# Products with w1 read the first norm's transposed tile, with the second norm's factor per token applied behind them

## The chip, the cores and the metric

The kernel runs on one core of a Trainium2 chip. Its time is the device time of one execution in microseconds (us). Five engines work side by side, each in the order of its own queue: TensorE (PE, matrix products, with the weight loads listed as PEld), VectorE (DVE), ScalarE (ACT), GpSimd (POOL) and SyncE (SP, which here issues most DMA transfers). They wait for one another by semaphores.

## What is computed

x holds 2,048 tokens of 512 values. It is normalised once (xn), and xn goes two ways: through an attention with 32 heads of 16 in four segments of 512 tokens, and through an MLP of width 1,792 that normalises xn a second time.

```
def _A_ref(x, wq, wk, wv, wo, beta):
    ...
    for s in range(N):
        qs, ks, vs = q[:, :, s], k[:, :, s], v[:, :, s]
        logits = jnp.einsum("bhqd,bhkd->bhqk", qs, ks) * scale + mask
        p = _softmax(logits, axis=-1)
        a_dot = jnp.einsum("bhqk,bhkd->bhqd", p, vs)
        pq = phi(qs)
        num = jnp.einsum("bhld,bhde->bhle", pq, M)
        den = jnp.einsum("bhld,bhd->bhl", pq, z)[..., None] + 1e-6
        o = g * (num / den) + (1.0 - g) * a_dot
        ...
    return o @ wo

def _B_ref(x, w1, b1, w2, b2):
    y = _layernorm(x, axis=-1)
    h = _gelu(jnp.einsum("bsd,df->bsf", y, w1) + b1)
    return jnp.einsum("bsf,fd->bsd", h, w2) + b2

xn = _layernorm(x, axis=-1)
return x + _A_ref(xn, ...) + _B_ref(xn, ...)
```

A row of xn already has mean zero. Its second norm is therefore xn times one number per token, which depends on the variance of the row of x alone.

## The kernel before

Precision: every float32 operand of the large products is split into two float16 parts, high and low, and a product is the sum of three (high-high, high-low, low-high), so `split3` (L499) issues 12 products for a contraction over 512.

Work is cut into segments of 512 tokens (s, 0 to 3), groups of 8 heads (g, 0 to 3; i = 4s + g counts 16 of them), halves of 256 tokens (hf, 0 to 7) and halves of the hidden width (fh; j = 2 hf + fh counts 16 MLP stages of 7 blocks of 128 columns).

The jobs that the prediction speaks of:

- `ln` (L462) and `ln_out` (L477). For kind "X" they load two token tiles of x, compute the statistics on DVE (`norm_stats`), apply them on POOL or ACT (`norm_apply`), transpose them on PE (four transposes for each tile, L490) and split them into `xnT[s]`, one buffer for 512 tokens. For kind "Y" they load the same tiles of x again, compute the statistics again, apply both norms at once (the second pair in `stats`), and transpose into `yT`, a tile for 256 tokens.
- `qk_proj` (L517): projection of a group's queries or keys, 12 products of 512 columns, read out by ACT and by DVE (`qk_low`), stored to memory, and reloaded by `qk_rows` in another layout (`qst`, `kst`).
- `m_job` (L637): score products whose row maxima DVE takes (L653); `m_row` (L657) transposes the maxima, stores them (`md`) and `max_rows` adds them to `qst`. `s_job` (L677): the scores again, with the maximum subtracted, and their exponentials on ACT (L695, `pt`). `s_mask` masks on POOL, `pv` (L716) multiplies with the values, `o_norm` divides.
- `d_jobs` (L773): a block of 128 hidden columns for 256 tokens, 12 products of 256 columns with `yT`; the result is scaled and b1 added while it is read from PSUM, on ACT for even blocks and on DVE for odd ones (`Z_ON`), into `hT`. `gelu` (L790): one ACT instruction over the seven blocks, 1,792 columns. `h_split` (L795) splits the result, and `e_jobs` (L815) multiply with w2.
- `out_jobs` (L840): the products with wo. `v_nat` (L606): the values.

PSUM has eight banks of 512 float32 columns. Which bank a job takes is written out in `BANKS`, and the order in which all jobs are issued in `ORDER`: one character for each job, which names the stream (`streams`, L58) whose next job follows. Each engine gets its instructions in that order. ACT needs one table set for exponentials and another for the gelu; `plan` (L167) places the reloads, one before and one after each of the 16 gelu stages.

Of the kernel before, what the change touches and what calls it, by code (L numbers as in the profile page):

```python
# [19 lines left out]
P = 128  # L20
# [30 lines left out]
Z_ON = "AVAVAVA"  # L51
# [6 lines left out]
def streams():  # L58
# [76 lines left out]
    "egaeaaeRgeaRTTaTTeaaRTebeebScbbTcfXXTUecSUhVdeegXdijUUZWZZe3lZm001y0YY0k21k23l0ImI1I30IVeoY0o21IIeY44e52IJ4Ao6"  # L135
    "o54hKNcWo4Le6Oo75ioA4AoMkKooL764P75PMUjVKkLAP7o6Mz7#nPKLUyPM8PP89!Po8ppP9WII8!8NqppoIeqPopoqX#O#I8rr9rreop!oPP"
    "89Ip!opIpqo#IoopPccqz#rrqrJrod$$%$KdP$shInp&%Ni&pIjLaMlmt$aqkpp$kuqplvI%IqIyIwo(eoxor$rrrpPmPKLIppoaM&KzqPoL%p"
    "OohMqoopPPiaK(qP&koLJMoKrr(LrMrPPsPKojtbkbIPLnIP(PMKPIupopLIDvI)wPpqoMapNIopoPPxqaqyKPIrrLOrarppoPPzoaMo*oJPKP"
    "bPbPL)qPcP+MP)copohipjpPoPcd*dqlnCqyrKm)rrrLpppsq+MhkIItuIkpoKpvwIELqPiFqDooMKrrrxrGLPIjPPoppHlpoMpPPPIpokoICq"
    "qPIPmJoookqrrrKrPAPLPsootnooAuPopvMpwxPqAppqpAEoorrqrrKpopBpooBpQLMqpKcNqcoBoPnBLqrrrrpcpzsytquhvjPMpOKipFpPGq"  # L140
    "IHlQzmIDwqIxrrCNrLrppOpMkkPPPIIpoqoPIdydpooEqahoiQooJqkrrrrsPPIKLMIPotKuovoPPLPFIPIPjowMGKLxHMKlILNPnmkIPMpppa"
    "PIPqPOzPPoJaopaPPPbKqICPLMpooPbPqrQKLrrMroDopIIopoIKLPNPMaIpppaqIqKLEIqooararrrPPJosbybtMPPPOunhvPpppjccFiPGcw"
    "HPPqpKqpqPLPlxkmdMzdrrrCKrppPyhpLkppDjqIiEIqIoqorMrrroosoKAAtooIAuvowoFoGHIxLkloBICMInKPpmpQkApppPPqqPzPLcJqoo"
    "oDrrrrBpMpoPPKLyoopBppohooqMqorqrrriBPPoIsntjEPPQPuPvppFGpHkwcKILlzmPqMPPNpkpCKqxILQINIyrrqrrMoopPDIIKpoPdcOLo"
    "ppMPqOPPqpooPPqdPoJKaorrLrroosMhIEiKLtMQuNIPPvojFKIGLkHPPPnMlPPmwKIppIPLqxPppMpPCazIPykIoqaJooqPPrKDrrrooLMoPN"
    "KPIbILpapoPPPbPppaoMPPoqpoOOqPaIrKrqrrosaEaLMKIIInPtbbIcuLpppvPhpFcipcDGqHqldCMmPdPPwPPqJrrxrKkrcpppPkPhPEiqIo"
    "ppLzIqooqorrrMKrsPAooLMKotuvIAocwooFLPIGMHlIICIoKPnxBAAmpppLkBPkooqphPopMoQPJqPiPPrqKrrroooPPBppLMKoPNIOpoqPPQ"
    "oDLpNpBoIIMqqrKrrLrnppsqpMtcIKIIIEupvpFPwLOPqGHqlmPdCdxPJPkrrMrrppPkPPPKPPopLoqMPPIpKpqoIqPorrrLMDrsoooKEtuhIP"
    "PQiIvPoLMoFoKQLwGPkHlmIMoIIJPPDKPLMPPInCkIpKpqoxPPpoPPppoqILooqrrrropPpMoNKqIppoqLIooMNpKILOIorrqrrsMJnPKPtOPE"
    "upppPPppPPvwqLPqqPrFxrrrpMKpGPPPLqPMKpppPHLqPPPqMrrrKLrsMPPtPPPPuPvPwPxPPBBBBQQQQ"  # L150
# [4 lines left out]
    "01234567012345601274350617243150627341502734015273401576340123470162347062134076213407612340761243607124731602"  # L155
    "47316524763015247630524763052467310246170234610724671204671254361725431672453016742350617452061207465120746352"
    "40673540267315420731654273164527136527136075123062531064251032641703264170326417304173265041732650417326045173"
    "20645173245061725407612407561240561724056172406517243605127403612740326740326710452610452610453610543617043561"
    "72043175620147356214735162473516243750243175043217043521670432156701432657014321657043216570432167543210754321"
    "07542310754231072534610374256104237610423760452376045236145723614527345612735461352476015324701532470152470315"  # L160
    "67031564703154672031546723154673215421673052310673521067235016723501672530167524316752430617542310675423106542"
    "35106423510645210643521064352130564103564720356472037526403527106435271063452671043526710325674103264710326043"
    "721560403721506472150647150632715207631205726031572601357426013754021637524106375410637542106754210367154"
# [17 lines left out]
def infini_mixer_kernel(ctx: ExitStack, tc: tile.TileContext, x, wq, wk, wv, wo, beta, w1, b1, w2, b2, out):  # L181
# [240 lines left out]
    stats = cst.tile([P, S // P, 2, 2], F32, name="stats")  # L422

    def norm_stats(tok, tiles):


        n = len(tiles)
        ag = sm.tile([P, 4, 2], F32, name="ag", bufs=1)[:, :n]
        for j, t in enumerate(tiles):
            st = sm.tile([P, 6], F32, name="st")  # L430
            V.bn_stats(st, t)
            V.bn_aggr(ag[:, j, :], st)
        w = sm.tile([P, 3, 4, 2], F32, name="nw", bufs=1)[:, :, :n]
        a, y, b = w[:, 0], w[:, 1], w[:, 2]
        r = stats[:, tok:tok + n]
        V.tensor_scalar(a[:, :, 0], ag[:, :, 1], EPS, None, op0=OP.add)
# [5 lines left out]
        q = r[:, :, :, 0]  # L442
# [6 lines left out]
        for j in range(2):  # L449
            V.scalar_tensor_tensor(r[:, :, j, 1], ag[:, :, 0], -1.0, r[:, :, j, 0], op0=OP.mult, op1=OP.mult)  # L450

    def norm_apply(tok, tiles, twice, act, j):
        for t in tiles[j:j + 1]:
            a, b = stats[:, tok + j, twice, 0:1], stats[:, tok + j, twice, 1:2]
# [7 lines left out]
    def ln(kind, n, b, part):  # L462

        tok = 4 * n + 2 * b if kind == "X" else 2 * n
        if part == 0:
            lt[kind, n, b] = ts = []
            for j in range(2):
                name = ("nN", "nD")[j] if (kind, n, b) == ("X", 0, 1) else "xt"
# [3 lines left out]
        elif part == 1:  # L472
            norm_stats(tok, lt[kind, n, b] + (lt[kind, 0, 1] if n == 0 else []))
        else:
            norm_apply(tok, lt[kind, n, b], kind == "Y", (kind, n, b) == ("X", 0, 1), part - 2)

    def ln_out(kind, n, b, k):  # L477
        if kind == "X":
            if n not in xnT:
                xnT[n] = sb.tile([P, KT, 2, SEG], F16, name="xnT")  # L480
            ln_tr(lt["X", n, b][k], xnT[n], 256 * b + P * k)
        else:
            if n not in yT:
                yT[n] = sb.tile([P, KT, 2, 256], F16, name="yT")
            ln_tr(lt["Y", n, b][k], yT[n], P * k)

    def ln_tr(t, dst, c0):
# [8 lines left out]
    xnT = {}  # L496
    yT = {}

    def split3(p, parts, n, s0, s1):  # L499

        (ws, wsl), (xs, xsl) = parts
        i = 0
        for k in range(n):
            for a, b in ((0, 0), (0, 1), (1, 0)):
                T.matmul(p, wsl(ws, k, a), xsl(xs, k, b), start=s0 and i == 0, stop=s1 and i == 3 * n - 1)  # L505
# [11 lines left out]
    def qk_proj(i, which):  # L517
# [3 lines left out]
        split3(p, ((w, lambda w, k, a: w[:, g, a, P * k:P * k + P]),  # L521
                   (xnT[s], lambda t, k, a: t[:, k, a, :])), KT, True, True)
# [83 lines left out]
    def v_nat(s, b):  # L606
        p = dense()
        split3(p, ((xnT[s], lambda t, k, a: t[:, k, a, P * b:P * b + P]),
                   (wvs, lambda w, k, a: w[:, k, a, :])), KT, True, True)
# [163 lines left out]
    def d_jobs(j):  # L773
        hf, fh = divmod(j, 2)
        hz = hzs[fh]

        def f(fi):
            def go():
                fo = FH * fh + fi
                p = dense()  # L780
                split3(p[:, :256], ((WT["1"], lambda w, k, a: w[:, fo, a, P * k:P * k + P]),
                                    (yT[hf], lambda t, k, a: t[:, k, a, :])), KT, True, True)
                if Z_ON[fi] == "A":
                    A.activation(hz[:, fi, :], p[:, :256], AF.Identity, bias=b1t[:, fo:fo + 1], scale=col(CG + fh))  # L784
                else:
                    V.tensor_scalar(hz[:, fi, :], p[:, :256], col(CG + fh), b1t[:, fo:fo + 1], op0=OP.mult, op1=OP.add)  # L786
            return go
        return [f(fi) for fi in range(FH)]

    def gelu(j):  # L790
        A.activation(hzs[j % 2], hzs[j % 2], AF.Gelu_apprx_tanh)  # L791
# [100 lines left out]
    def e_of(j, a, f):  # L892
# [8 lines left out]
        "X": lambda *k: ln("X", *k), "Xt": lambda *k: ln_out("X", *k),  # L901
        "Y": lambda *k: ln("Y", *k), "Yt": lambda *k: ln_out("Y", *k), "gate": gates,
        "D": lambda j, f: once("D", j, lambda: d_jobs(j))[f](),
# [38 lines left out]
```

## Time and profile before

| | us |
|---|---|
| median of three runs | 722.24 |
| the three runs | 720.87, 722.24, 722.72 |
| the profiled execution | 720.38 |
| its span, first to last instruction | 718.7 |

The profile is one execution. In its lists, a line gives the place in the kernel (L505 is line 505, often that of a helper), the engine, the operation, the tiles out<-in, the size, and the count; then the busy time in us and the mean of one in ns; then the idle time of the engine just before such instructions and what ended most of it. A list of waits gives the engine and line that waited, for whom, the us in total, how often, and the longest. A timeline gives start, duration, engine, line and tiles, with the idle time in brackets. The duration of a product includes its way through the array, which overlaps the next one; the pace is read from the starts.

### The profile page before, as it was taken

What the parts mean: (1) busy time and instruction counts of PE and PEld (TensorE: products, weight loads), DVE (VectorE), ACT (ScalarE), POOL (GpSimd) and SP (SyncE); (2) the same over time, 40 slices, a digit from 0 to 9 for tenths busy, and PEclk for the clock granted to TensorE, in tenths of its full rate; (3) what the DMA queues carried; (4) which work ended last, traced back from release to release, by engine and by line L of the source; (5) the groups of instructions that cost most, each with busy time, mean ns of one, the idle gap of its engine ahead of it and who ended that gap; (6) DMA issues with size and microseconds to landing.
All of it is one profiled execution on the core that took longest, in us unless ns stands there. A gap on an engine that the chain in (4) does not pass through costs nothing.

```text
span 718.7 us, 14578 instructions
## 1 busy us (share of the span) xinstructions
PE 689.8 (96%) x5189; PEld 379.0 (53%) x5189; DVE 524.3 (73%) x1677; ACT 519.7 (72%) x908; POOL 352.9 (49%) x544
## 2 busy tenths in 40 slices
PE   2799999999999999999999999999999999999997
PEld 2365655564554465665555456556556455455543
DVE  5799877988786659897485866888658484696642
ACT  5989998889767577578936757676864567748980
POOL 3568746655514462654533336445634245334572
PEclk9999999999999999999999999999999999999999
DMA  9886124503220163322313024322240321322101
GB/s 266 242 255 157 53 79 108 127 16 92 52 68 3 61 148 89 82 53 55 96 31 90 16 66 113 92 60 60 68 104 2 97 67 17 82 68 68 32 1 59
DMA packets 54084, 59.16 MB, mean 82 GB/s; under 512 B 5038, under 2 KB 40892, under 8 KB 54012
## 3 DMA queue, kind: packets, MB, share of 16 engines
q1 hardware_dynamic: 51708, 54.04, 27.0%
q0 software_dynamic: 2304, 4.20, 3.6%
q8 instruction: 41, 0.67, 0.4%
q14 instruction: 31, 0.25, 0.1%
HBM read 41.18 MB, written 17.04 MB: 81 GB/s over the span
## 4 chain that ended last, share of the span: by engine, by line
PE 84%; DMA 5%; ACT 5%; DVE 2%; issue 2%; SPq 1%; POOL 0%; POOLq 0%; DVEq 0%; ACTq 0%
PE dense L505 33%; PE dense L831 19%; PE dense L722 9%; PE dense L646 6%; PE dense L688 5%; PE dense L849 5%; DMA qst<-qd 2%; DMA qd<-hl 2%; PE dense L601 2%; PE dense L589 1%; PE dense L621 1%; PE dense L490 1%; ACT pt L695 1%; DMA pt<-in_A_wq_dram 1%; PE dense L562 1%
## 5 line engine op out<-in xcount | busy, mean ns | idle before, releaser
L653 DVE CUSTOM_DVE_ANT_0 dense<-dense,mask 128x384 f32<-128x384 f32 (+3 forms) x512 | 234.0, 524 | 37.9 <-PE dense L646 35.8
L695 ACT ACTIVATE pt<-dense,qkcs 128x512 f32<-128x512 f32 (+1 forms) x384 | 204.4, 628 | 28.0 <-PE dense L688 27.9
L831 PE MATMUL dense<-w2s,hT 128*128 128x512 f16 x672 | 165.3, 380 | 0.0
L505 PE MATMUL dense<-yT,w1s 128*128 128x256 f16 x1344 | 160.5, 273 | 1.8 <-POOL w1s L413 1.4
L709 POOL TENSOR_SCALAR_AFFINE_SELECT pt<-pt 128x256 f32<-128x256 f32 x256 | 102.7, 443 | 104.5 <-ACT pt L695 104.0
L505 PEld LDWEIGHTS <-w1s 128*128 128x128 f16 x1344 | 129.5, 98 | 34.7 <-issue 9.9
L805 POOL TENSOR_TENSOR hT<-hh,hT 128x512 f16<-128x512 f32 x64 | 69.5, 1086 | 64.6 <-ACT hT L803 61.9
L831 PEld LDWEIGHTS <-hT 128*128 128x128 f16 x672 | 60.9, 98 | 71.3 <-issue 16.7
L722 PE MATMUL dense<-pt,vt 128*32 128x512 f32 (+3 forms) x1024 | 76.3, 436 | 0.0
L653 DVE DVE_READ_ACCUMULATOR2_ANT mc<- 128x1 f32 x512 | 71.9, 140 | 0.0
L801 POOL TENSOR_SCALAR hh<-hT,sc 128x512 f32<-128x512 f32 x64 | 43.4, 679 | 46.7 <-ACT hT L791 43.6
L784 ACT ACTIVATE hT<-dense,b1t,sc 128x256 f32<-128x256 f32 x64 | 36.7, 573 | 37.8 <-PE dense L505 37.3
L753 POOL TENSOR_TENSOR nN<-nN,oT 128x512 f32<-128x512 f32 x16 | 20.5, 1280 | 73.8 <-DVE oT L574 73.8
L646 PE MATMUL dense<-kst,qst 48*128 48x384 f16 (+3 forms) x512 | 52.7, 298 | 3.8 <-DMA qst<-qd 3.8
L722 PEld LDWEIGHTS dense<-pt,vt 128*32 128x32 f32 x1024 | 30.9, 109 | 45.2 <-issue 33.4
L688 PE MATMUL dense<-qst,kst 50*128 50x384 f16 (+3 forms) x512 | 52.1, 298 | 2.1 <-DMA qst<-md 1.7
L505 PE MATMUL dense<-xnT,wks 128*128 128x512 f16 x192 | 45.6, 388 | 0.0
L505 PE MATMUL dense<-xnT,wqs 128*128 128x512 f16 x192 | 44.1, 379 | 0.0
L849 PE MATMUL dense<-wos,oT 128*128 128x512 f16 x192 | 43.8, 379 | 0.1
L505 PE MATMUL dense<-wvs,xnT 128*128 128x512 f16 x192 | 43.6, 379 | 0.0
L803 ACT ACTIVATE hT<-hh 128x512 f16<-128x512 f32 x64 | 37.4, 584 | 7.4 <-POOL hh L801 7.4
L786 DVE TENSOR_SCALAR hT<-dense,sc,b1t 128x256 f32<-128x256 f32 x48 | 25.9, 539 | 23.0 <-PE dense L505 22.8
(223 smaller groups left out, 931.5 us busy)
## 6 DMA issues: line engine op xcount, KB each, us to landing
xt<-in_A_x_dram SPq DMA_DIRECT2D x30, 256.0 KB
kd<-hl SPq DMA_DIRECT2D x48, 128.0 KB
qd<-hl SPq DMA_DIRECT2D x48, 128.0 KB
kst<-kd SPq DMA_DIRECT2D x32, 192.0 KB
qst<-qd SPq DMA_DIRECT2D x32, 192.0 KB
acc<-in_A_x_dram SPq DMA_DIRECT2D x16, 256.0 KB
acc<-in_B_b_dram POOLq DMA_DIRECT2D x16, 256.0 KB, 4.1
out_dram<-acc SPq DMA_DIRECT2D x16, 256.0 KB
```

The costliest lines, as they stand in the source:

```text
L505: T.matmul(p, wsl(ws, k, a), xsl(xs, k, b), start=s0 and i == 0, stop=s1 and i == 3 * n - 1)
L646: T.matmul(p[:, o:o + n], stk[i, 0][r, t, P * qb:P * qb + P], stk[i, 1][r, t, :n], start=True, stop=True)
L653: V.tensor_tensor_reduce(p[:, o:o + n], p[:, o:o + n], mask[:, 512 - n:], 1.0, -3e38, OP.add, OP.max, mc[i][:, 4 * b + t, qb:qb + 1])
L688: T.matmul(p[:, o:o + n], stk[i, 1][r, t, P * kb:P * kb + P], stk[i, 0][r, t, P * kb:], start=True, stop=True)
L695: A.activation(pt[i, 4 * b + t][:, OFF[kb]:OFF[kb] + n], p[:, c:c + n], AF.Exp, scale=qkcs[:, 1, i % NG:i % NG + 1])
L709: G.affine_select(v, v, pattern=[[0, 2], [1, P]], compare_op=OP.is_ge, fill=0.0, base=0, channel_multiplier=-1)
L722: T.matmul(p[32 * c:32 * c + 32, P * kb:], vt[s, kb][:, 4 * g + c, 16 * odd:16 * odd + 32], pt[i, 2 * c + odd][:, OFF[kb]:OFF[kb] + LEN[kb ...
L801: G.tensor_scalar(hht[j, c], hz[:, z, :], col(SHH + j % 2), 0.0, op0=OP.mult, op1=OP.add)
L803: A.activation(hT[:, z, 0, :], hht[j, c], AF.Copy)
L805: G.tensor_tensor(hT[:, z, 1, :], hht[j, c], hT[:, z, 0, :], op=OP.subtract)
L831: T.matmul(p, t[:, u, P * a:P * a + P], w2s[:, fo, v, :], start=fi == 0 and n == 0, stop=fi == FH - 1 and n == 2)
L849: T.matmul(p, o[:, u, P * b:P * b + P], wos[:, g, v, :], start=i == 0, stop=i == 3 * NG - 1)
```

## The change

The second transposed tile is gone. The products with w1 read the first norm's tile, and what the second norm would have multiplied each token's row with, one factor per token, is applied when the products are read from PSUM.

- The streams "again" and "againt" (second load, statistics, norm and transposes) become "ratio" and "ratio2". `ratio` works out the factor for the 256 tokens of a half from what `norm_stats` left (two small DVE products) and stores it to memory; `ratio_rows` loads it back as a row of 256 that stands in all 128 partitions (`cb`, one buffer).
- `xnT` becomes a ring of three halves of 256 tokens. A segment's two halves are neighbours in it for segments 0, 2 and 3, not for segment 1, whose query and key projections are issued as two times 12 products of 256 columns (`x_seg`).
- Two blocks of w1 products share one PSUM bank, and one DVE instruction multiplies both with the scale and with the factors. The last of the seven blocks stands alone.
- b1 is added inside the gelu, as its bias column, which takes one ACT instruction for each block, seven in place of one.
- The first loads change place (x first), and `ORDER` and `BANKS` are written anew.

```diff
-Z_ON = "AVAVAVA"
...
-    for n in range(2 * NSEG):
-        put("again", *[("Y", n, 0, k) for k in (0, 2, 3)])
-        put("againt", *[("Yt", n, 0, k) for k in range(2)])
+    for h in range(2 * NSEG):
+        put("ratio", ("C", h))
+        put("ratio2", ("Cb", h))
...
-    stats = cst.tile([P, S // P, 2, 2], F32, name="stats")
+    stats = cst.tile([P, S // P, 2], F32, name="stats")
+    nws = {}
...
+    def ratio(h):
+
+        w, o = nws[2 * h]
+        a, q = w[:, 0, o:o + 2], w[:, 3, o:o + 2]
+        t = sm.tile([P, 2], F32, name="cr", bufs=1)
+        V.tensor_tensor(t, a[:, :, 0], q[:, :, 0], op=OP.mult)
+        V.tensor_tensor(t, t, q[:, :, 1], op=OP.mult)
+        Q.dma_start(cd[h].rearrange("t p -> p t"), t)
+
+    def ratio_rows(h):
+        cbt[h] = sb.tile([P, 256], F32, name="cb")
+        Q.dma_start(cbt[h], bass.AP(tensor=cd[h].tensor, offset=cd[h].offset, ap=[[0, P], [1, 256]]))
...
+    xnT = cst.tile([P, 3, KT, 2, 256], F16, name="xnT")
+
+    def ln_out(n, b, j):
+        t, dst, c0 = lt[n, b][j], xnT[:, (2 * n + b) % 3], P * j
...
+    def x_seg(s):
+
+        a, b = 2 * s % 3, (2 * s + 1) % 3
+        if b == a + 1:
+            return [(slice(0, 512), lambda k, u: xnT[:, a:a + 2, k, u, :])]
+        return [(slice(256 * j, 256 * j + 256), lambda k, u, h=h: xnT[:, h, k, u, :]) for j, h in enumerate((a, b))]
...
-    def d_jobs(j):
+    dp = {}
+
+    def d_job(j, f):
         hf, fh = divmod(j, 2)
...
+        fo = FH * fh + f
+        if f % 2 == 0:
+            dp[0] = dense()
+        p = dp[0]
+        split3(p[:, 256 * (f % 2):256 * (f % 2) + 256], lambda k, a: WT["1"][:, fo, a, P * k:P * k + P],
+               lambda k, a: xnT[:, hf % 3, k, a, :])
+        if f % 2 or f == FH - 1:
+            f0, n = f - f % 2, 1 + f % 2
+            V.scalar_tensor_tensor(hzs[fh][:, f0:f + 1, :], p[:, :256 * n].rearrange("p (f c) -> p f c", f=n), col(CG + fh),
+                                   cbt[hf].unsqueeze(1).to_broadcast([P, n, 256]), op0=OP.mult, op1=OP.mult)
 
     def gelu(j):
-        A.activation(hzs[j % 2], hzs[j % 2], AF.Gelu_apprx_tanh)
+        for f in range(FH):
+            fo = FH * (j % 2) + f
+            A.activation(hzs[j % 2][:, f, :], hzs[j % 2][:, f, :], AF.Gelu_apprx_tanh, bias=b1t[:, fo:fo + 1])
```

More of the change, by code (lines that the diff above doesn't have):

```diff
@@ L472, in ln @@
         elif part == 1:
-            norm_stats(tok, lt[kind, n, b] + (lt[kind, 0, 1] if n == 0 else []))
+            norm_stats(tok, lt[n, b] + (lt[0, 1] if n == 0 else []))
         else:
[L475 to L487, printed above, removed]
+            norm_apply(tok, lt[n, b], (n, b) == (0, 1), part - 2)
+    xnT = cst.tile([P, 3, KT, 2, 256], F16, name="xnT")
+    def ln_out(n, b, j):
+        t, dst, c0 = lt[n, b][j], xnT[:, (2 * n + b) % 3], P * j
         p = dense()
@@ L494, in ln_tr, with x_cols, split3 @@
         V.scalar_tensor_tensor(dst[:, :, 1, c0:c0 + P], p3, 1024.0, h, op0=OP.mult, op1=OP.subtract)
[L496 to L501, printed above, removed]
+    def x_seg(s):
[3 more added lines that the diff above has]
+        return [(slice(256 * j, 256 * j + 256), lambda k, u, h=h: xnT[:, h, k, u, :]) for j, h in enumerate((a, b))]
+    def x_cols(s, b, k, u):
+        return xnT[:, (2 * s + b // 2) % 3, k, u, P * (b % 2):P * (b % 2) + P]
+    def split3(p, ws, xs):
         i = 0
-        for k in range(n):
+        for k in range(KT):
             for a, b in ((0, 0), (0, 1), (1, 0)):
-                T.matmul(p, wsl(ws, k, a), xsl(xs, k, b), start=s0 and i == 0, stop=s1 and i == 3 * n - 1)
+                T.matmul(p, ws(k, a), xs(k, b), start=i == 0, stop=i == 3 * KT - 1)
                 i += 1
@@ L607, in v_nat @@
         p = dense()
[L608 to L609 removed]
+        split3(p, lambda k, a: x_cols(s, b, k, a), lambda k, a: wvs[:, k, a, :])
         t = vts[b]
```

98 lines of the change are left out of this document (44 added, 54 removed).

## The prediction

> **What bounds the kernel now.** I read the page's busy times first, then the table by stage, then what TensorE (PE) waits for, then the timeline of a quiet stretch.
>
> ```profile
> PE 689.8 (96%) x5189; PEld 379.0 (53%) x5189; DVE 524.3 (73%) x1677; ACT 519.7 (72%) x908; POOL 352.9 (49%) x544
> ...
> PEclk9999999999999999999999999999999999999999
> ```
>
> PE is busy for 689.8 of 718.7 us at a full granted clock. A busy PE need not be a PE at its peak, so the next rows matter more. The columns of the table by stage are the stage, then busy time and count for PE, weight loads, DVE, ACT and POOL, then clock, DMA share and GB/s.
>
> ```profile
> 0.00:20.00 20.00, 6.01 (x24) 4.77 (x25) 11.23 (x47) 12.31 (x27) 7.69 (x21) 1.00 0.91 267
> 20.00:40.00 20.00, 15.36 (x94) 9.38 (x93) 15.83 (x50) 18.53 (x32) 12.13 (x13) 1.00 0.75 224
> ...
> 300.00:320.00 20.00, 20.00 (x171) 11.99 (x170) 17.00 (x66) 16.69 (x27) 10.32 (x17) 1.00 0.38 92
> ...
> 600.00:620.00 20.00, 18.89 (x132) 9.70 (x129) 10.14 (x12) 18.29 (x30) 11.75 (x18) 1.00 0.36 78
> ```
>
> In the first 20 us DMA is the full resource (0.91), in the next 20 ACT (18.53). Later PE fills the stage, with a small hole at 600. What the holes are:
>
> ```profile
> PE dense L490 <- POOL xt L458: 7.4, 1, 7.4
> PE dense L359 <- ACT wqs L343: 6.4, 2, 5.6
> PE dense L646 <- DMA qst<-qd: 3.8, 5, 1.1
> PE dense L376 <- ACT w1s L343: 3.1, 1, 3.1
> PE dense L688 <- DMA qst<-md: 1.7, 1, 1.7
> PE dense L505 <- POOL w1s L413: 1.4, 1, 1.4
> ```
>
> The 7.4, 6.4, 3.1 and 1.4 are the start. After it, PE waits 5.5 us (3.8 + 1.7) for two DMA chains. Whether it is at its peak between them shows in the starts of neighbouring jobs:
>
> ```profile
> 300.62 1.47 PE L505 MATMUL dense<-yT,w1s 128*128 128x256 f16 x12
> 301.93 1.46 PE L831 MATMUL dense<-w2s,hT 128*128 128x512 f16 x6
> ...
> 306.26 2.12 PE L831 MATMUL dense<-w2s,hT 128*128 128x512 f16 x9
> 308.22 0.60 PE L490 MATMUL dense<-ident,xt 128*128 128x128 f32 x4
> 308.65 1.47 PE L505 MATMUL dense<-yT,w1s 128*128 128x256 f16 x12
> ```
>
> Twelve products of 256 columns take 301.93 - 300.62 = 1.31 us (109 ns each), nine of 512 take 308.22 - 306.26 = 1.96 us (218 ns each): the pace follows the columns and no weight load shows. Four transposes take 308.65 - 308.22 = 0.43 us. So from about 36 us on, time is PE's own work, and only an edit to that work, or to the 5.5 us of waits, is on the path.
>
> **PE's work, part by part.** The second norm's tile is gone: 8 halves of two 128-token tiles, so 16 groups of four transposes, 16 x 0.43 = **-6.9 us**. The products with w1 keep count and shape (1,344 of 256 columns): 0. In the ring, segment s lies in slots 2s and 2s+1 modulo 3; only segment 1 lies in slots 2 and 0. There the 8 query and key projections split from 12 products of 512 columns into 24 of 256. A 512-column projection takes 2.59 us (606.48 to 609.07, quoted below), the split one 2 x 1.31 = 2.62: 8 x 0.03 = **+0.2 us**. The other segments, and the value products, which read 128 columns at a time, keep their shapes.
>
> **What lies beside PE.** The rows that price it:
>
> ```profile
> L784 ACT ACTIVATE hT<-dense,b1t,sc 128x256 f32<-128x256 f32 x64 | 36.7, 573 | 37.8 <-PE dense L505 37.3
> ...
> L791 ACT ACTIVATE hT<-hT 128x1792 f32<-128x1792 f32 x16 | 27.2, 1698 | 0.2
> ...
> L786 DVE TENSOR_SCALAR hT<-dense,sc,b1t 128x256 f32<-128x256 f32 x48 | 25.9, 539 | 23.0 <-PE dense L505 22.8
> ...
> L458 POOL TENSOR_SCALAR xt<-xt,stats 128x512 f32<-128x512 f32 x30 | 24.0, 802 | 18.0 <-DVE stats L450 6.3 <-PE dense L505 4.5 <-DVE wks L407 3.7
> L835 DVE SCALAR_TENSOR_TENSOR acc<-dense,sc,acc 128x512 f32<-128x512 f32 x32 | 23.9, 746 | 18.8 <-PE dense L831 18.5 <-DMA qd<-hl 0.2
> ...
> L791 ACT ACT_TABLE_LOAD x16 | 20.5, 1283 | 0.3
> ...
> L494 DVE SCALAR_TENSOR_TENSOR yT<-dense,yT 128x512 f16<-128x512 f32 x16 | 10.8, 682 | 3.9 <-ACT yT L493 3.9
> L431 DVE BATCH_NORM_STATS2 st<-xt 128x6 f32<-128x512 f32 x14 | 9.4, 674 | 5.8 <-DMA xt<-in_A_x_dram 5.8
> L493 ACT ACTIVATE yT<-dense 128x512 f16<-128x512 f32 x16 | 9.1, 601 | 0.7 <-PE dense L490 0.7
> ...
> L803 ACT ACTIVATE hT<-hh 128x256 f16<-128x256 f32 x16 | 6.8, 423 | 2.5 <-POOL hh L801 2.5
> ```
>
> ```profile
> 300.86 0.17 DVE L436 TENSOR_SCALAR nw<-ag 128x2 f32<-128x2 f32 x1
> ...
> 303.37 0.23 DVE L450 SCALAR_TENSOR_TENSOR stats<-ag,stats 128x2 f32<-128x2 f32 x2
> ```
>
> DVE loses the 48 reads of L786 (25.9), the 16 of L494 (10.8), and eight repeats of the statistics: two reads of 0.67 and a chain of 303.60 - 300.86 = 2.7, about 4.1 each, 33. It gains 64 products with the factor per token: 48 of 512 columns at L835's 0.746 and 16 of 256 at L786's 0.54, 44.4, and 16 small ones at 0.17 for the factor: 2.7. Net 47.1 - 69.7 = -23 us. The new form (PSUM times a row repeated over two blocks) is not in the trace; below, 0.539 for a plain 512-column read would be kind, above, a quarter over 0.746 costs 9 us more and still leaves DVE under its present load. I take 0.746, the same operation.
>
> ACT loses L784 (36.7), L493 (9.1) and 16 wide gelus (27.2), and gains 112 gelus of 256 columns with a bias column. Their price lies between L803's 0.423 (same size, SBUF, no column) and L784's 0.573 (PSUM, two columns): 47 to 64 us; I take 0.45, nearer the SBUF row, 50, net -23. POOL loses 16 x 0.80 = 12.8. The cover is that PE reads none of these directly. If it is gone, each gelu stage is 7 x 0.423 - 1.70 = 1.3 to 7 x 0.573 - 1.70 = 2.3 us longer with ACT closed to everything else. Against that, the wide gelu starts only when all seven products are read; a slice starts when its own two are, so behind the last product remain a DVE read, one slice and the table reload, 0.54 + 0.45 + 1.28 = 2.3, where there were 0.57 + 1.28 + 1.70 + 1.28 = 4.8. In the order string the gelu now mostly stands 0 to 5 us behind its last product, formerly up to 17. I take 0.
>
> The Trainium skill speaks against the slices: "ScalarE: Activation LUTs", section "What ACT_TABLE_LOAD costs", gives an activation with a bias column a fixed 280 ns and 0.833 ns per column, and 186 ns fixed without it. By it the wide gelu is an estimated 1.68 us, with which the row (1.698) agrees, and seven slices 3.45 us; that is inside the bounds above, leaves the sum, and would make the slower rival below 16 x 1.8 = 28 us instead of its 21.
>
> **Queues and added waits.** SP issues 16 second reads of x less and 16 small transfers more: the factors of a half are stored to memory and come back repeated over all partitions. The load back waits on SP for its store, and for the last DVE product of the half before, as it has one buffer; behind it wait the projection stores and reloads that feed the maximum products. The nearest row for such a pair is the maxima's round trip:
>
> ```profile
> SPq L669 <- DMA md<-mhl: 18.5, 15, 2.2
> ```
>
> That is 18.5 / 15 = 1.2 us mean. In the new order most factors are stored some 30 us of PE work or more ahead of the load, so I take 0; eight full waits would be 10 us of SP, not of PE. Of the ring: the tile of half h+3 overwrites that of half h, so its copies on ACT and DVE now wait for the w1 jobs of half h too. In the new string these stand 55 us of PE work ahead at the least, so 0; out of order they would hold the next segment's projections. Two w1 jobs share a PSUM bank, so their read starts up to 1.31 us later; the bank's next use stands no nearer behind it than before (0.65 us at the least in both strings): 0.
>
> **The new order.** I laid both strings out with PE prices from the rows. Two places where PE waited:
>
> ```profile
> 589.74 0.27 PE L659 MATMUL dense<-ident,mc 128*32 128x128 f32 x1
> ...
> 596.65 0.98 PE L688 MATMUL dense<-qst,kst 50*128 50x512 f16 x8 [1.73 <-DMA qst<-md]
> ...
> 606.48 2.75 PE L505 MATMUL dense<-xnT,wqs 128*128 128x512 f16 x12
> 609.07 0.81 PE L831 MATMUL dense<-w2s,hT 128*128 128x512 f16 x3
> ...
> 611.98 2.36 PE L722 MATMUL dense<-pt,vt 128*32 128x512 f32 x32
> 614.27 0.61 PE L688 MATMUL dense<-qst,kst 50*128 50x512 f16 x6
> 614.81 4.06 PE L831 MATMUL dense<-w2s,hT 128*128 128x512 f16 x18
> ...
> 620.89 0.39 PE L646 MATMUL dense<-kst,qst 48*128 48x512 f16 x1 [0.53 <-DMA qst<-qd]
> ```
>
> From the end of a query projection (609.07) to its maximum products (620.89) the chain needs 11.8 us. The old string put 9.5 us of PE work between them; the new one puts three w1 jobs, nine of w2, one value group and two score jobs there: 3.93 + 5.85 + 2.29 + 0.54 = 12.6. The shortest such distance over the 16 groups is 8.7 in the old, 10.9 in the new. From the maxima's transpose (589.74) to the scores (596.65) the chain needs 6.9; the old string had 4.9 there, the new one 6.8, least 5.6 against 4.1. So of the 5.5 us of waits I take **-4**, with bounds of -5.5 and 0. A new order can also place new waits that I don't see: **+2**, from 0 to 8.
>
> **The start.** x is now read ahead of the first weights, and the second read is gone:
>
> ```profile
> 14.72 1.16 SPq L470 DMA_DIRECT2D xt<-in_A_x_dram  x2
> ...
> 18.95 4.19 PE L505 MATMUL dense<-xnT,wks 128*128 128x512 f16 x12
> ```
>
> The row at 14.72 stood ahead of w1: 0.5 MB at 267 GB/s is 1.9 us. The first weights come 1 MB, 3.9 us, later, the norms 1.9 earlier. The first projection (18.95) needs both. I take **-1**, from -3 (norms and w1 both earlier, within the 4.5 us of L376's and L413's waits) to +4 (all of the weights' delay).
>
> **Sum.** 718.7 - 6.9 + 0.2 - 4 + 2 - 1 = 709.0 us of span; with the 1.7 us around it (720.38 - 718.7) 710.7. The profiled execution lies 1.9 under the median of the runs, so 712.6 against 722.24. The likeliest case's own range is 707 to 717.
>
> **Rivals.** (1) More: waits wholly gone, no new ones, start -3: 722.24 - 6.9 + 0.2 - 5.5 - 3 = 707. For it, the wider distances; against it, the old string had such waits at distances that looked long enough.
> (2) Given back: the new order's waits come to 8 and the old ones change places (0 gained): 722.24 - 6.7 + 8 - 1 = 722.5. For it, DVE alone now reads the w1 products, and it is near full at places (17.00 of 20 at 300); against it, it carries 23 us less.
> (3) Slower: the slices hold ACT, the scores' exponentials queue behind them, their PSUM banks stay taken and PE stops at the next score job. With 1.3 us exposed in all 16 stages, 712.6 + 20.8 = 733. It decides from 12 us on, that is from nine stages. For it, the score jobs that in the new string follow three gelus within 3 us; against it, the earlier start of the slices.
> (4) That the transposes stood in time that PE would have waited anyway is excluded by the rows at 306 to 308, which touch.
>
> **Chances.** Forecast 0.60, (1) 0.12, (2) 0.12, (3) 0.16. Differences within 0.3% (2.2 us) can hardly be told from no change here. (2) is half of that kind and splits the rest: faster 0.75, same 0.06, slower 0.19. The range, 705 to 723, leaves out (3) and the ends of the others.
>
> **What would show it.** No transposes of xt beyond the first norm's 64 and PE's work about 6.7 us less; waits for qst under 2 us; ACT's gelu rows near 0.45 us and no PE wait on L695; DVE's busy time near 500. PE waits for ACT's or DVE's readers of PSUM adding to over 10 us would prove the forecast wrong, as would a first projection later than 22 us.

## The result and the profile after

The changed kernel takes 742.28 us (median of 4 runs, 741.61 to 746.31) against 721.56 us (4 runs, 719.76 to 722.72) of the kernel before in the same session: 1.0301 times, 95% interval 1.0258 to 1.0345. The forecast was 712.6, so the sign was wrong. The profiled execution spans 739.9 us where before it was 718.7.

The page of the changed kernel, busy times, granted clock (tenths of full speed in 40 slices) and packets:

```profile
PE 700.2 (95%) x5221; PEld 383.9 (52%) x5221; DVE 528.8 (71%) x1693; ACT 501.1 (68%) x924; POOL 338.9 (46%) x528
...
PEclk9989999999999999999999899999899999999999
...
DMA packets 55110, 56.04 MB, mean 76 GB/s; under 512 B 7086, under 2 KB 43964, under 8 KB 55036
```

PE is busy 10.4 us longer than before (689.8), though 64 transposes are gone, and three slices of the clock show an 8 where there was none. Outside its busy time PE idles 739.9 - 700.2 = 39.7 us, before 718.7 - 689.8 = 28.9. The table by stage says where (stage, then busy time and count of PE, weight loads, DVE, ACT, POOL, then clock, DMA share, GB/s):

```profile
20.00:40.00 20.00, 13.44 (x47) 5.39 (x47) 11.16 (x44) 12.73 (x22) 5.71 (x6) 0.85 0.77 162
100.00:120.00 20.00, 17.61 (x127) 10.24 (x126) 12.90 (x37) 15.31 (x28) 9.48 (x14) 0.91 0.26 73
280.00:300.00 20.00, 18.35 (x141) 10.73 (x140) 17.27 (x49) 11.30 (x21) 5.30 (x12) 0.91 0.27 63
300.00:320.00 20.00, 20.00 (x152) 14.21 (x151) 14.91 (x45) 10.92 (x21) 10.16 (x11) 1.00 0.48 135
400.00:420.00 20.00, 16.78 (x117) 7.50 (x115) 8.85 (x29) 8.39 (x16) 3.11 (x8) 0.83 0.17 47
520.00:540.00 20.00, 16.17 (x93) 8.32 (x86) 10.05 (x18) 12.63 (x24) 5.75 (x7) 0.83 0.11 29
```

The stage at 300 is as full as before. The loss lies in a few places, the start among them (13.44 us of PE work at 20 to 40, 15.36 before). At 400 and 520 the other engines do less as well and DMA moves little (47 and 29 GB/s): what is waited for is neither large nor starved, but late. (The stage at 280 has another cause, which the last experiment takes up.) The waits of PE and of SP's queue in the changed kernel (engine, line, for whom, us in total, times, longest):

```profile
PE dense L704 <- DMA qst<-md: 7.3, 3, 3.7
...
SPq L685 <- DMA md<-mhl: 27.2, 13, 6.8
...
SPq L468 <- DMA cd<-cr: 16.2, 2, 8.8
```

Before, SP's longest wait for the maxima's store was 2.2 us; now it is 6.8. SP waits up to 8.8 us for the new store of the factors (`cd`). The timeline of the changed kernel shows what the two have in common:

```profile
27.39 0.42 SPq L464 DMA_DIRECT2D cd<-cr  x1
27.86 0.45 SPq L311 DMA_DIRECT2D w2s<-in_B_w_dram  x1
37.17 0.34 SPq L468 DMA_DIRECT2D cb<-cd  x1
...
98.60 0.38 SPq L464 DMA_DIRECT2D cd<-cr  x1
106.47 0.33 SPq L468 DMA_DIRECT2D cb<-cd  x1
...
521.47 0.38 SPq L464 DMA_DIRECT2D cd<-cr  x1
...
523.37 0.33 SPq L680 DMA_DIRECT2D md<-mhl  x1
...
530.57 0.56 SPq L685 DMA_DIRECT2D qst<-md  x2
...
532.26 1.99 PE L704 MATMUL dense<-qst,kst 50*128 50x512 f16 x8 [3.69 <-DMA qst<-md]
```

At 98.60 the factors are stored and come back at 106.47, 7.9 us later. At 521.47 they are stored again, and 1.9 us behind them the maxima; now the maxima need 7.2 us (523.37 to 530.57), though the load of the factors only stands behind them. So the store is late itself and what is issued behind it is late too. At the start the store at 27.39 comes back 9.8 us later (37.17), and a load of weights goes out right behind it. The stage of 30 to 32 us, in the changed kernel and in the version with rows below (t_rows), which has the same load at 27.61:

```profile
30.00:32.00 2.00, 2.00 (x9) 0.83 (x9) 1.56 (x12) 1.37 (x2) 0.00 (x0) 0.69 1.34 32
```

```profile
30.00:32.00 2.00, 2.00 (x7) 0.72 (x6) 1.70 (x12) 1.09 (x4) 0.86 (x2) 0.52 0.96 363
```

The DMA share is high in both (1.34 and 0.96), but what moves is 32 GB/s behind the scattered store and 363 without it: data are held up, and not only the news that they have landed. The first products with w1 start at 38.30 there, at 33.22 in t_rows.

At 530 PE pays twice. Stages of the changed kernel around that place, same columns:

```profile
524.50:529.50 5.00, 4.07 (x20) 1.67 (x18) 3.09 (x7) 2.83 (x5) 2.48 (x3) 1.00 0.03 3
529.50:532.50 3.00, 0.24 (x1) 0.09 (x1) 0.43 (x1) 0.00 (x0) 1.37 (x2) 1.00 0.04 7
532.50:539.40 6.90, 6.76 (x22) 3.23 (x22) 1.69 (x3) 5.32 (x9) 0.00 (x0) 0.51 0.25 77
```

PE stands still for most of 3 us, and then works 6.9 us at a granted clock of 0.51: another 3.4 us lost without any wait in a list (after 539.4 the clock is full again). Over the span, the clock's mean of 0.979 makes 0.021 x 739.9 = 15 us of it.

### The profile page after: what moved, and what is told of

It is laid out like the page before. It is cut to its first block, busy times and chain, and to the rows that moved or that the text cites. A ratio compares the mean times of both kernels' runs of the same rounds, so it can differ in the third digit from the quotient of the medians.

```text
span 739.9 us, 14673 instructions
## 1 busy us (share of the span) xinstructions
PE 700.2 (95%) x5221; PEld 383.9 (52%) x5221; DVE 528.8 (71%) x1693; ACT 501.1 (68%) x924; POOL 338.9 (46%) x528
## 4 chain that ended last, share of the span: by engine, by line
PE 71%; DMA 8%; ACT 6%; issue 5%; DVE 5%; POOL 4%; SPq 1%; POOLq 0%; ACTq 0%; DVEq 0%
PE dense L522 29%; PE dense L847 14%; PE dense L738 8%; PE dense L865 5%; PE dense L662 5%; PE dense L704 5%; DMA md<-mhl 2%; DMA kd<-hl 2%; DMA qst<-qd 1%; ACT pt L711 1%; PE dense L618 1%; PE dense L606 1%; PE dense L637 1%; DMA wqs<-in_A_wq_dram 1%; PE dense L579 1%
## 5 line engine op out<-in xcount | busy, mean ns | idle before, releaser
L522 PE MATMUL dense<-xnT,w1s 128*128 128x256 f16 x1344 | 166.4, 276 | 5.6 <-ACT w1s L410 3.9
L847 PE MATMUL dense<-w2s,hT 128*128 128x512 f16 x672 | 169.1, 384 | 0.3 <-ACT pt L711 0.2
L801 DVE SCALAR_TENSOR_TENSOR hT<-dense,sc,cb 128x512 f32<-128x512 f32 x64 | 43.4, 680 | 37.6 <-PE dense L522 33.1
L704 PE MATMUL dense<-qst,kst 50*128 50x384 f16 (+3 forms) x512 | 54.4, 301 | 7.8 <-DMA qst<-md 7.3
L662 PE MATMUL dense<-kst,qst 48*128 48x384 f16 (+3 forms) x512 | 54.4, 302 | 4.6 <-DMA qst<-qd 1.8
L542 ACT ACTIVATE hl<-dense 128x512 f16<-128x512 f32 x32 | 19.1, 598 | 46.0 <-PE dense L522 32.5
L807 ACT ACTIVATE hT<-hT,b1t 128x256 f32<-128x256 f32 x112 | 47.2, 496 | 4.3 <-DVE hT L801 3.8
L522 PE MATMUL dense<-xnT,wqs 128*128 128x512 f16 (+1 forms) x240 | 47.3, 352 | 0.0
L522 PE MATMUL dense<-xnT,wks 128*128 128x512 f16 (+1 forms) x240 | 46.2, 347 | 1.0 <-ACT wks L405 1.0
```

The lines of the kernel that those rows point to most:

```text
L522: T.matmul(p, ws(k, a), xs(k, b), start=i == 0, stop=i == 3 * KT - 1)
L662: T.matmul(p[:, o:o + n], stk[i, 0][r, t, P * qb:P * qb + P], stk[i, 1][r, t, :n], start=True, stop=True)
L704: T.matmul(p[:, o:o + n], stk[i, 1][r, t, P * kb:P * kb + P], stk[i, 0][r, t, P * kb:], start=True, stop=True)
L801: V.scalar_tensor_tensor(hzs[fh][:, f0:f + 1, :], p[:, :256 * n].rearrange("p (f c) -> p f c", f=n), col(CG + fh), cbt[hf].unsqueeze(1).to ...
L807: A.activation(hzs[j % 2][:, f, :], hzs[j % 2][:, f, :], AF.Gelu_apprx_tanh, bias=b1t[:, fo:fo + 1])
L847: T.matmul(p, t[:, u, P * a:P * a + P], w2s[:, fo, v, :], start=fi == 0 and n == 0, stop=fi == FH - 1 and n == 2)
```

## The experiments

My theory: the store of the factors, 256 pieces of 4 B in the order "t p -> p t", is late, and holds what is issued behind it. Rivals: the new order, and the gelu slices. The first four runs tell them apart. Two of them leave the second norm's factor out, as their expectations say.

**The factors as rows (t_rows).** DVE transposes the factors in blocks of 32, so that a store has pieces of 128 B. Everything else, order, slices and ring, is that of the changed kernel.

```diff
-        t = sm.tile([P, 2], F32, name="cr", bufs=1)
+        w = mst[:, 3] if h < 2 else ones
+        t, r = w[:, 0:2], w[:, 32:64]
...
-        Q.dma_start(cd[h].rearrange("t p -> p t"), t)
+        V.transpose(r, w[:, 0:32])
+        for c in range(2):
+            Q.dma_start(cd[h][c].rearrange("(b k) -> b k", k=32), r[c:P:32, :])
```

> The changed kernel, but the factors of a half are transposed on DVE in blocks of 32 and stored as eight pieces of 128 bytes in place of 256 pieces of 4 bytes. In the profile of the changed kernel the scattered store at 98.60 us let its reload go only at 106.47, and the maxima stored at 523.37, right behind another such store, could be read back only at 530.57, 7 us instead of the usual 1.5. Theory A (the scattered store completes some 7 us late and holds what is behind it): the waits of PE for the maxima fall from 7.3 us to under 2, the drops of the granted clock behind them go, time 719 to 729. Rival B (the new order is short of distance whatever the store is): 739 to 745, the same waits. Rival C (the gelu slices hold ACT): also 739 to 745.

Measured: 713.1 us (4 runs, 711.87 to 714.83), 0.9913 of the kernel before (0.9881 to 0.9944), 6 us under the expected range. Page and timeline of this kernel:

```profile
PE 689.4 (97%) x5221; PEld 380.3 (53%) x5221; DVE 530.6 (74%) x1701; ACT 501.0 (70%) x924; POOL 338.9 (48%) x529
```

```profile
90.71 1.09 SPq L467 DMA_DIRECT2D cd<-mst  x2
93.56 0.33 SPq L471 DMA_DIRECT2D cb<-cd  x1
```

Store to reload takes 2.9 us instead of 7.9, and PE waits for no `qst` at all. PE's busy time falls by 10.8 us (the clock) and its idle time from 39.7 to 713.1 - 689.4 = 23.7 us, 16.0 less; the two make the 26.8 us between the spans. Order and slices are unchanged here, so neither is the cause of the loss.

**The store without its use, and without itself (store_only, no_store).** Both load the rows of `cb` from b1; the second issues no store.

```diff
# store_only
-        Q.dma_start(cbt[h], bass.AP(tensor=cd[h].tensor, offset=cd[h].offset, ap=[[0, P], [1, 256]]))
+        Q.dma_start(cbt[h], bass.AP(tensor=b1.tensor, offset=b1.offset, ap=[[0, P], [1, 256]]))
# no_store, besides
-        Q.dma_start(cd[h].rearrange("t p -> p t"), t)
```

> The changed kernel with the scattered stores as they are, but the rows of factors are loaded from b1 in place of the stored factors (the second norm's factor is left out of the result), so nothing waits for a store's completion by name. Theory A in its wide form (what is issued behind the store is held too): the late reload of the maxima at about 523 to 531 us and of the queries behind the store at about 400 us stay, time 732 to 742. Theory A in its narrow form (only the reload that waits for the store, and SP's queue behind that wait, are late): 722 to 732. Rivals B and C: 739 to 745.

> The changed kernel without the eight scattered stores, rows of factors loaded from b1 (the second norm's factor is left out of the result). This takes the store away without the DVE transposes of the kernel that stores in rows. Theory A, wide or narrow: 718 to 728, the granted clock full after the start but for the place at about 282 us, where DVE waits for POOL. Rivals B and C: 739 to 745.

Measured in one run each: 737.67 us, in the range of the wide form, and 713.86 us, 4 us under the expected range. SP's waits for the maxima's store, first with the unread store, then without any:

```profile
SPq L685 <- DMA md<-mhl: 29.4, 13, 6.9
```

```profile
SPq L684 <- DMA md<-mhl: 18.8, 13, 2.6
```

The unread store costs 737.67 - 713.86 = 23.8 us. Waiting for the factors themselves is about the rest, 742.28 - 737.67 = 4.6 us; single runs stand behind both figures.

**The same store in the kernel before (before_store).** Eight scattered stores that nothing reads:

```diff
+    cd = [dr.tile([2, P], F32, name=f"cd{h}") for h in range(2 * NSEG)]
...
+            if kind == "Y" and part == 2:
+                Q.dma_start(cd[n].rearrange("t p -> p t"), stats[:, tok:tok + 2, 0, 0])
```

> The kernel before with eight scattered stores of the same form added, one for each half, of the norm's factors that stand in its statistics; nothing reads them. No other edit, the old order. Theory A, wide: each store holds the transfers behind it for some 7 us, and where a chain through memory has less to spare PE waits: time plus 5 to 20 us. Theory A, narrow, and rivals B and C: within 2 us of the kernel before.

Measured: 737.96 us (4 runs), 1.0256 times the kernel before (1.0223 to 1.0289). A wait and a stage of this kernel:

```profile
PE dense L376 <- ACT w1s L343: 11.4, 1, 11.4
```

```profile
20.00:40.00 20.00, 8.57 (x39) 4.98 (x38) 8.31 (x31) 10.44 (x18) 6.07 (x6) 0.67 0.82 187
```

Eight transfers of 1 KB cost 16 to 21 us (the interval times 719.7) in another kernel, a large part of it at the start, where the weights' loads stand behind the first ones: PE is busy 8.57 us of the stage instead of 15.36. The fault needs nothing else of the change.

**What makes the store late (store_apart, store_pairs).** Both are store_only with another layout in memory: the 256 pieces of 4 B each 512 B apart, or 128 pieces of 8 B side by side.

```diff
# store_apart
-    cd = [dr.tile([2, P], F32, name=f"cd{h}") for h in range(2 * NSEG)]
+    cd = [dr.tile([P, 2, 128], F32, name=f"cd{h}") for h in range(2 * NSEG)]
...
-        Q.dma_start(cd[h].rearrange("t p -> p t"), t)
+        Q.dma_start(cd[h][:, :, 0], t)
# store_pairs
-    cd = [dr.tile([2, P], F32, name=f"cd{h}") for h in range(2 * NSEG)]
+    cd = [dr.tile([P, 2], F32, name=f"cd{h}") for h in range(2 * NSEG)]
...
-        Q.dma_start(cd[h].rearrange("t p -> p t"), t)
+        Q.dma_start(cd[h], t)
```

> The kernel store_only with the 256 pieces of 4 B written 512 B apart instead of 4 B apart. If the pieces are late because they write into the same stretch of memory one after another, the lateness goes: 712 to 720 us. If the number of pieces sets it, it stays at 734 to 740 us.

> The kernel store_only (stores made, reload replaced by rows of b1, factor left out; 737.7 us) with a store of 128 pieces of 8 B, each in one place per partition, instead of 256 of 4 B. If the number of small pieces sets the lateness, about half of it goes: 722 to 730 us. If pieces of less than some size conflict in the same stretch of memory, 734 to 740 us. If it is the transposed layout alone, 712 to 717 us.

Measured in one run each: 708.67 and 711.42 us, both under the lowest range of their expectations. Their waits for the maxima's store:

```profile
SPq L685 <- DMA md<-mhl: 18.8, 13, 2.3
```

```profile
SPq L685 <- DMA md<-mhl: 17.5, 13, 2.0
```

The number of pieces is not it: 256 pieces of 4 B cost nothing that shows when they lie apart. The same place in each run says it most plainly, the maxima stored 1.9 us behind the last store of factors: they come back after 7.2 us in the changed kernel, 7.4 in store_only, 1.4 in store_apart, 1.9 in store_pairs, and 1.4 in no_store, where nothing stands ahead of them. The transposed layout alone, the third case of store_pairs, is not it either: store_apart keeps the two pieces of a partition 512 B apart, as in the late store, and moves only those of neighbouring partitions away from each other. What is left is pieces of 4 B from neighbouring partitions side by side in the same few hundred bytes. Whether 8 B do better because there are half as many or because each is larger, these runs don't separate. Why store_apart lies 5 us under no_store, the last experiment bears on.

**Which queue is held (store_act, before_store_act).** The scattered store goes out from ACT's queue, first in store_only, then in before_store.

```diff
-        Q.dma_start(cd[h].rearrange("t p -> p t"), t)
+        A.dma_start(cd[h].rearrange("t p -> p t"), t)
```

> The kernel store_only with the same scattered store issued from ACT's queue instead of SP's. If the late store holds only what is issued behind it on its own queue, SP's transfers go free and the time is 712 to 718 us, with PE waits for qst as in no_store. If it holds the DMA engines for every queue, it stays at 732 to 740 us.

> The kernel before with the eight scattered, unread stores of before_store (737.96 us from SP's queue), now issued from ACT's queue, where the data they store are ready. If a late store holds only what is behind it on its own queue, PE's waits for qst are those of before (3.8 us for qst from qd) and the time is 719 to 725 us. If it holds every queue, 732 to 740 us.

Measured: 728.03 us (one run), and 747.62 us (4 runs; 1.0398 of before, 1.0362 to 1.0433). The first falls between its two cases and is confounded: ACT's queue now stands until DVE has made the factors, behind its reads of the w1 products (the store goes out at 510.50), as ACT's next row shows:

```profile
510.91 0.69 ACT L608 ACTIVATE rc<-dense,qkcs 128x512 f32<-128x512 f32 x1 [5.48 <-DVE hT L801]
```

The second issues its stores where the data are ready. ACT's waits for the projections' store, which SP's queue issues, in the kernel before, in before_store and in before_store_act:

```profile
ACT hl L525 <- DMA kd<-hl: 1.8, 2, 1.1
```

```profile
ACT hl L528 <- DMA kd<-hl: 6.0, 3, 3.5
```

```profile
ACT hl L528 <- DMA kd<-hl: 10.8, 3, 6.8
```

The longest of them in the timeline of before_store_act:

```profile
530.31 0.58 SPq L541 DMA_DIRECT2D kd<-hl  x1
...
530.68 0.37 ACTq L478 DMA_DIRECT2D cd<-stats  x1
...
539.60 0.60 ACT L528 ACTIVATE hl<-dense 128x512 f16<-128x512 f32 x1 [6.84 <-DMA kd<-hl]
```

A transfer on SP's queue keeps ACT waiting for 6.84 us though the scattered store went out on ACT's queue, and 0.4 us later than the transfer. The other two such waits (until 178.63 and 360.05) also end some 10 to 12 us behind a scattered store. PE's waits for qst from qd, which the expectation named, say less: 4.1 us in total against 3.8, the longest 2.6 against 1.1. So the store holds more than its own queue, and another queue is no way out. The Trainium skill, "DMA: Bandwidth & Descriptors", section "Queues, rings and completion order", says of the write that counts up a transfer's semaphore that it lands only after every earlier write of that DMA engine, across its queues. That fits these waits, though not by itself the slow data at 30 to 32 us; no run here shows the write itself.

**The order of before (old_order).** t_rows issued in the order of the kernel before as far as its steps allow, with the bank string written anew.

> The changed computation (first norm's tile shared, factor brought behind, factors stored as rows of 128 B) issued in the order of before as far as its new steps allow. If the computation alone gives the gain of t_rows (16 x 0.43 us fewer transposes), it lands at 711 to 716 us beside t_rows at 713.1. If the order of the steps carries part of the gain, it stays at 717 to 723 us, no better than before. Where the order of before makes the new steps wait, PE waits of over 3 us for one tile show it.

Measured: 820.71 us (4 runs), far outside both cases. Waits and a stage of this kernel:

```profile
PE dense L666 <- DVE mc L673: 12.6, 4, 4.1
...
PE dense L666 <- DMA qst<-qd: 10.4, 8, 4.2
```

```profile
200.00:300.00 100.00, 76.62 (x487) 35.48 (x486) 47.13 (x160) 42.32 (x79) 22.22 (x42) 0.87 0.07 20
```

The waits are spread over many lines, some of over 4 us, and PE stands idle for nearly a quarter of this stage. This transcription of the old order doesn't fit the new computation; it doesn't say what the order alone is worth, and that stays open.

**Is the transposes' gain on the path? (t_rows_twice)** Each of the 64 transposes issued twice, the count of before:

```diff
-        for k in range(KT):
+        for k in 2 * list(range(KT)):
             T.transpose(p[:, P * k:P * k + P], t[:, P * k:P * k + P], ident)
```

> The kernel t_rows (713.1 us) with each of the 64 transposes of the norm's tiles issued twice into the same place, which is the number of transposes of the kernel before. The prediction prices a group of four at 0.43 us on PE: 16 groups would bring 6.9 us back, to 718 to 722 us. If the transposes lay beside other work, 712 to 715 us. If their gain went through ACT and DVE instead (evacuations, which this kernel does not repeat), 712 to 715 us too.

Measured: 718.16 us (10 runs), 0.9972 of before (0.9955 to 0.999) where t_rows had 0.9913: 5.1 us by the medians, 4.2 by the two ratios, of the 6.9 that the prediction priced. Page of this kernel:

```profile
PE 692.7 (97%) x5285; PEld 386.6 (54%) x5285; DVE 530.8 (74%) x1701; ACT 501.6 (70%) x924; POOL 339.0 (47%) x529
```

The gain goes through PE: its busy time is 3.3 us longer than in t_rows, and some 1.4 us are to be added, since the mean granted clock is 0.995 here and 0.993 there. A repeated group of four costs 0.44 us where PE is busy (eight transposes from 503.53 to 504.40), as priced. But 4 of the 16 groups stand before 19 us, where PE waits for loads and norms anyway: the first products with w1 start no later with them (32.44 us) than without (33.22). The other 12 make 12 x 0.43 = 5.2 us, which fits the medians. So a group's price holds, but only where PE is not waiting. Two of the 16 groups that the prediction counts stood ahead of such a wait as well (at 22.97 and 23.66 in the kernel before, with PE's wait until 30.00 behind them), so -6.0 would have been nearer than -6.9.

**Pairs with the factor applied (after_pairs).** The layout of store_pairs, the row read by DVE with a stride of two in two instructions.

```diff
-            V.scalar_tensor_tensor(hzs[fh][:, f0:f + 1, :], p[:, :256 * n].rearrange("p (f c) -> p f c", f=n), col(CG + fh),
-                                   cbt[hf].unsqueeze(1).to_broadcast([P, n, 256]), op0=OP.mult, op1=OP.mult)
+            for t in range(2):
+                c = slice(P * t, P * t + P)
+                V.scalar_tensor_tensor(hzs[fh][:, f0:f + 1, c], p[:, :256 * n].rearrange("p (f c) -> p f c", f=n)[:, :, c], col(CG + fh),
+                                       cbt[hf].rearrange("p (c t) -> p t c", t=2)[:, t:t + 1, :].to_broadcast([P, n, P]),
+                                       op0=OP.mult, op1=OP.mult)
```

> The changed kernel with its factors laid down as 128 pieces of 8 B, one per partition, and read back as one row; DVE reads the row with a stride of two, in two instructions per pair of tiles (64 more on DVE, some 12 us of DVE work). If the layout of the 4 B pieces was the whole fault, 710 to 716 us, level with t_rows at 713.1 or a little under it, with each reload issued within 3 us of its store. If halving the pieces only halves the lateness, waits of 3 to 4 us from store to reload and 718 to 730 us. If DVE's extra work reaches PE, PE waits for hT at the lines of w2.

Measured: 717.43 us (12 runs, 713.63 to 721.62), 0.9961 of before (0.9938 to 0.9983), between the two expected ranges. SP's wait for the factors' store, and the page:

```profile
SPq L468 <- DMA cd<-cr: 6.6, 2, 4.2
```

```profile
PE 691.5 (96%) x5221; PEld 380.8 (53%) x5221; DVE 538.3 (75%) x1757; ACT 501.9 (70%) x924; POOL 339.8 (47%) x528
```

The longest wait is 4.2 us instead of 8.8, but that is not half of everything. Two reloads stand right behind their stores. From store to reload the first takes 5.2 us (27.37 to 32.53; 9.8 in the changed kernel, 2.6 in t_rows), the second 2.8 (96.48 to 99.32; 7.9 and 2.9). So pairs are late at the start, where much else is loaded, and not at the second place. Whether the start or the 7.7 us more of DVE makes the 4 us to t_rows was not separated.

**A stall that the store does not make (t_rows_pool).** In t_rows one piece of the span runs at half clock, behind a hole (stages as above):

```profile
268.00:272.50 4.50, 2.41 (x20) 1.37 (x18) 4.50 (x4) 3.58 (x7) 3.34 (x8) 0.99 0.33 54
272.50:279.30 6.80, 6.28 (x38) 2.01 (x36) 6.17 (x23) 2.32 (x4) 0.00 (x0) 0.50 0.18 60
```

In its timeline POOL adds b2 to a tile of x (`acc`) whose load was issued at 261.08, and DVE waits behind POOL. The same stall in the changed kernel, the second list here, is what the stage at 280 showed:

```profile
265.73 0.89 POOL L833 DMA_DIRECT2D acc<-in_B_b_dram  x1 [5.67 <-ACT pt L715]
...
267.86 2.91 DVE L602 TENSOR_SCALAR zr<-bd,zst 128x128 f32<-128x128 f32 x1 [4.04 <-POOL mst L649]
```

```profile
279.66 0.89 POOL L829 DMA_DIRECT2D acc<-in_B_b_dram  x1 [4.83 <-DMA acc<-in_A_x_dram]
```

The first row puts POOL's wait down to ACT, the last one to the load; the run below decides.

One character of the order string is moved 15 steps on:

```diff
-    "lrQxmNrrMCrOppIIkqzpDkpaqpQPPIbPcIooorrqrrPPJdPPsoooPIKtyLhuQvPiMEKooNFLMGIHkKlmLPPooIwIPCMKPPoLkbIPznMaIOIPPJ"
+    "lrQxmNrrMCrppIIkqzpDkpaqpQOPPIbPcIooorrqrrPPJdPPsoooPIKtyLhuQvPiMEKooNFLMGIHkKlmLPPooIwIPCMKPPoLkbIPznMaIOIPPJ"
```

> The kernel t_rows (713.1 us) with one step moved: the addition of b2 to the sixth token tile, for which POOL waits for a load at 262 to 266 us, is issued 15 steps later, behind POOL's work on mst, xt and pt. If that wait makes the half-clock piece that t_rows has there (6.8 us, 3.4 us of work lost, and DVE's and PE's waits of some 2 us), the piece goes and the time is 706 to 711 us. If the piece has another cause, it stays at 712 to 715 us.

Measured: 709.01 us (6 runs, 708.27 to 709.68), 0.9855 of the kernel before (0.983 to 0.9879). Stage and page of this kernel:

```profile
265.00:275.00 10.00, 10.00 (x86) 5.70 (x84) 8.20 (x25) 8.67 (x17) 4.04 (x9) 1.00 0.44 109
```

```profile
PE 685.0 (97%) x5221; PEld 379.3 (54%) x5221; DVE 528.6 (75%) x1701; ACT 501.3 (71%) x924; POOL 340.0 (48%) x529
```

Hole and half-clock piece are gone: 4.1 us for moving a step of POOL, whose wait reached PE only through DVE. no_store has a half-clock piece of 3.4 us at the same place (273 us) and store_apart has none, which is likely a part of the 5 us between them, two single runs. This is the fastest version, 33 us under the changed kernel.

## Why the prediction was wrong

**The step that failed** is the one on the queues: "most factors are stored some 30 us of PE work or more ahead of the load, so I take 0; eight full waits would be 10 us of SP, not of PE". It priced the factors' store by the row of the maxima's store, 1.2 us mean, because both are small stores that come back. The two have different forms: the scattered one takes 7.9 us from store to reload. The distances were as said (six of the eight loads stand 36 us or more behind their store), and yet the two that stand right behind it made SP wait 16.2 us, more than the 10 named for all eight. And it weighed the store only by who waits for it. The runs show the cost on what is issued behind it: 23.8 us with nobody reading it.

**The second price left out** was the clock. The wait of 3.69 us at 532.26 cost 3.4 us more after it. "+2, from 0 to 8" for new waits, and rival (2) with 8, both priced a hole at its length. The two signs that were to prove the forecast wrong, over 10 us of PE waiting for readers of PSUM and a first projection later than 22 us, did not come; they looked at other places than the store.

**The rivals** on the slow side named other mechanisms. The gelu slices came out at 496 ns:

```profile
L807 ACT ACTIVATE hT<-hT,b1t 128x256 f32<-128x256 f32 x112 | 47.2, 496 | 4.3 <-DVE hT L801 3.8
...
L801 DVE SCALAR_TENSOR_TENSOR hT<-dense,sc,cb 128x512 f32<-128x512 f32 x48 | 35.7, 746 | 32.9 <-PE dense L522 28.4 <-DMA cb<-cd 3.4 <-POOL pt L725 1.0
...
L801 DVE SCALAR_TENSOR_TENSOR hT<-dense,sc,cb 128x256 f32<-128x256 f32 x16 | 7.7, 480 | 4.8 <-PE dense L522 4.8
```

That is above my 0.45 and within its bounds. The prediction's estimate from the Trainium skill, "ScalarE: Activation LUTs", section "What ACT_TABLE_LOAD costs", 3.45 us for seven slices or 493 ns each, agrees with it. The slices don't make the loss: t_rows has them all, and there no wait of PE for ACT after the start is over 0.2 us. The new DVE form, bounded for want of a row, took the 746 ns that were taken for it, and 43.4 us in all where the prediction had 44.4.

**What held**, as t_rows shows, since it is the change without the late store: the way of the change, and two of its terms in the main. The transposes (-6.9 forecast) came to 5.1 when they were repeated; of the waits for `qst` (-4 forecast) none is left in t_rows, so -5.5. The new waits (+2) were the stall at 268 us, 4.1 us when it was taken out. That 713.1 lies so near the forecast of 712.6 is in part luck: the kernel before took 719.71 in that session, so the gain is 6.6 us where 9.6 were forecast. In the changed kernel itself the sign "waits for qst under 2 us" fell at once, with 7.3 on L704 alone. The start did not hold: -1 was forecast, and in the changed kernel the first projection starts at 19.89 instead of 18.95, within its bounds.

**DVE was wrong by 27 us and it cost next to nothing**: -23 forecast, 528.8 against 524.3 measured. I took eight repeats of the statistics out of the kernel before, and the description of it above says that it computes them again. It did not. The row that the prediction shows has 14 readings of `xt`, and the changed kernel has the same:

```profile
L431 DVE BATCH_NORM_STATS2 st<-xt 128x6 f32<-128x512 f32 x14 | 9.4, 673 | 2.6 <-DMA xt<-in_A_x_dram 2.6
```

A repeat would have shown as twice as many. "DVE's busy time near 500" was the sign to look for, and it fell at once. In t_rows, with 530.6 us of DVE, PE's only wait for DVE of over 0.5 us is one of 1.80 at 271.48, which belongs to the stall.

## What to carry to other kernels

Price a transfer by its form, the size of its pieces and where they fall, not by its bytes or by a neighbour of similar size, and ask what stands behind it on any queue before asking who reads it. A column of one value per partition that has to become a row is better transposed on the chip first: here that was worth 29 us for 8 KB. And a hole on PE can cost its length and then some microseconds at half clock (3.4 us lost after the hole at 530, nothing after a shorter one in the kernel before), so a short wait of an engine that PE never reads can be worth moving one step in the order.

## What the runs showed of the hardware

- A scattered store of 256 x 4 B into 1 KB took 7.9 us to come back (at 98.60), as rows of 128 B 2.9 us. Behind the one at 27.39 the DMA engines moved 32 GB/s at 30 to 32 us, against 363 with rows.
- Such a store holds other transfers, on other queues too, and one that was issued 0.4 us ahead of it (6.84 us on SP's queue, with the store on ACT's).
- After a stretch of the changed kernel with PE busy 0.24 of 3.0 us, and one of t_rows with 2.41 of 4.5, the granted clock was 0.51 and 0.50 for 6.9 and 6.8 us. The Trainium skill, "TensorE: Matmul & The Clock Gate", section "HAM oscillation — how this bites in real kernels", tells kernels to avoid gaps of over about 3.4 us. The 3.69 us of the changed kernel agree with that, t_rows does not: its longest single gap there is 1.80 us, and the 4.5 us hold 2.1 us of idle time in all. In the kernel before, a wait of 1.73 us, until 596.65, left the clock at full. Where between the two it turns was not tried.
